# Low parts of the output weights: on TensorE with plus and minus identity instead of on GpSimd, in a block-sparse attention and feed-forward kernel

## The chip, the cores and the metric

The kernel runs on one core of a Trainium2 chip. The metric is the time of one execution on the device in microseconds (us). The engines are TensorE (PE; PEld is its loading of weights), VectorE (DVE), ScalarE (ACT), GpSimd (POOL) and SyncE (SP), which here issues loads and stores. Each has its own queue of instructions and works through it in order; semaphores tie the queues together. SBUF is the memory that all of them read and write, PSUM the one that TensorE writes its products to.

## The reference

Attention over 4 batches of 8 heads, 768 positions, head size 64, in which a position sees only some of the 24 blocks of 32 keys; then a feed-forward layer with a rational function, on 3072 tokens of 512 numbers, 2048 hidden. Inputs and results are float32.

```
scores = scale * q @ k.T;  scores = where(mask, scores, -1e9)     # mask: neighbours, first, last, 3 sampled blocks
attn = exp(scores - max) / sum;  x = attn @ v                      # x: (3072, 512)
h = x @ w_in                                                       # (3072, 2048)
P = a[0] + a[1]*h + a[2]*h*h + a[3]*h*h*h
Q = 1.0 + abs(b[0])*abs(h) + abs(b[1])*h*h
out = (P / (Q + 1e-06)) @ w_out                                    # (3072, 512)
```

The weights come as float64 words, 1024 words of 32 bits for 512 numbers, and the kernel makes float32 of them with integer instructions.

## The kernel before, in words

**Units.** The tokens are cut into 12 chunks of 256 and the hidden dimension into 8 units of 256, so there are 96 units (c, u). A unit first multiplies its chunk with its input weights on TensorE (`into`, lines 1040 to 1042, 24 products into a PSUM tile `ph`), then ScalarE and VectorE evaluate the rational function from `ph` (lines 1047 to 1085), of which line 1057 on VectorE is the last to read `ph`. Two tiles come of it: `gh`, and the small rest `gl`. TensorE multiplies them with the output weights into `acc` (lines 1097, 1099, 1103). The order of the units is written in line 399.

**Output weights in three parts.** Each of the 16 tiles (128 hidden rows, 512 columns) of the output weights is needed as `wo_h` (fp32r, high part, line 1097), `wo_l` (bf16, what is left of the number after the high part, line 1099) and `wo_b` (bf16, short copy, line 1103). `one` (lines 424 to 492) makes them: SP loads the words (`wl`, line 432), an engine converts them (line 442), VectorE packs them into float32 in `dw` with three instructions (lines 446, 449, 453), then `out_high` copies `dw` to `wo_h` (line 463), `out_low` subtracts `wo_h` from `dw` into `wo_l` (line 469) and `out_short` copies `dw` to `wo_b` (line 466). Copies run through the helper `times` (lines 147 to 154), and so carry its lines: 150 on ScalarE, 152 or 154 on VectorE, 154 on GpSimd. `dw` has three buffers, `wl` two. The two `wo` tiles hold words of the input weights before (`homes`), so the last parts of their tile can be written only when those have been used.

**Who does what.** `issue` (lines 164 to 269) plans the program when it is built: it holds a list of operations (`Op`) with an engine, or several to choose from (`among`), a price in ns, what they follow, a priority and the buffers that they take, and writes them out in the order that its simulated clock gives. So a changed price or engine of one operation can move others on every engine. `out_high` may go to ScalarE (520), GpSimd (588) or VectorE (335), `out_low` to GpSimd (1225) or VectorE (602; none goes there), `out_short` to ScalarE alone. `Slot` and `Ring` (lines 103 to 114) stand for buffers. `r_ph` (line 274) has two: the tiles of the pool `ps_h` (line 85), which the units' `ph` use in turn.

**Fill.** While the planner finds TensorE idle in the first 80 us of its clock, it issues a product that nobody reads (`fill`, line 162).

**Attention.** TensorE makes scores (line 821), turns the probabilities with the identity (line 898) and multiplies them with the values (line 944). In the first batch GpSimd copies sampled key blocks (line 765). SP issues all loads (values lines 916 to 923, keys 779 to 785, output weights 432). `ident` is the float32 identity, `ident16` its f16 copy (lines 91 to 94).

## Time and profile before

| | |
|---|---|
| time, median of 3 runs | 824.07 us (822.8 to 828.83) |
| time of the profiled execution | 823.95 us |
| its span, first to last instruction | 821.9 us |
| mean granted TensorE clock | 0.987 |
| PE busy | 779.4 us (95%) |
| DVE busy | 670.1 us (82%) |
| ACT busy | 570.7 us (69%) |
| POOL busy | 76.2 us (9%) |

Shares are means over stages that differ. A table of stretches gives the busy time of each engine in a part of the span. The clock is the share of full speed that TensorE was granted (two levels, 1.2 and 2.4 GHz, so a mean of 0.93 is a mixture of 1 and 0.5). In the lists of groups, "busy us, mean ns" are the sum and the mean of one instruction, and behind the second bar stands the idle time of the engine just before them, and what ended it.

### The profile page before, as it was taken

How to read it: one execution, taken by the hardware profiler on the slowest of the kernel's cores; microseconds unless marked ns; L12 is line 12 of the kernel's file. 1: busy time of each engine (PE TensorE's matmuls, PEld its weight loads, DVE VectorE, ACT ScalarE, POOL GpSimd, SP SyncE). 2: the span in 40 equal slices, each digit the busy share in tenths (PEclk: the TensorE clock that was granted, in tenths of full speed). 3: DMA queues.
4: the chain of work that ended last, by engine and by line, in shares of the span. 5: the costliest groups of instructions: out<-in, count | busy, mean ns of one | idle time of the engine just before them, and what ended most of it. 6: DMA issues, size and time to landing. Idle time of an engine off the chain costs nothing.

```text
span 821.9 us, 27500 instructions
## 1 busy us (share of the span) xinstructions
PE 779.4 (95%) x10947; PEld 558.8 (68%) x10947; DVE 670.1 (82%) x1569; ACT 570.7 (69%) x1263; POOL 76.2 (9%) x128
## 2 busy tenths in 40 slices
PE   7889868799999998999999999999999999999997
PEld 3557545566677767677777767677777767777774
DVE  3779999999988883988777875887788886887886
ACT  2578785966866868676776759675776758767563
POOL 3416341333000000000000000000000000000000
PEclk9999997999999999999999999999999999999999
DMA  8988977437556746536546756535555446220000
GB/s 218 224 216 248 260 184 215 131 115 193 151 147 190 213 128 196 153 112 171 150 125 184 181 152 193 145 98 156 145 153 148 117 130 173 67 65 2 1 26 26
DMA packets 224415, 121.29 MB, mean 148 GB/s; under 512 B 62624, under 2 KB 214048, under 8 KB 224288
## 3 DMA queue, kind: packets, MB, share of 16 engines
q1 hardware_dynamic: 223136, 115.34, 51.2%
q0 software_dynamic: 1152, 4.19, 1.7%
q8 instruction: 87, 1.43, 0.7%
q14 instruction: 40, 0.33, 0.1%
HBM read 108.47 MB, written 11.01 MB: 145 GB/s over the span
## 4 chain that ended last, share of the span: by engine, by line
PE 78%; DVE 13%; ACT 3%; DMA 2%; issue 2%; SPq 1%; ACTq 0%
PE acc L1097 10%; PE ph L1040 9%; PE acc L1103 9%; PE acc L1099 9%; PE ph L1041 9%; PE ph L1042 9%; PE m L821 6%; PE av L944 6%; PE m L898 5%; PE acc L162 2%; PE m L555 2%; DVE pr L833 1%; PE m L982 1%; DVE dw L449 1%; DMA vg<-in_v_dram 1%
## 5 line engine op out<-in xcount | busy, mean ns | idle before, releaser
L1040 PE MATMUL ph<-xh,wi 128*128 128x256 f16 x768 | 211.6, 276 | 7.9 <-DVE tt L1057 7.9
L1041 PE MATMUL ph<-xl,wi 128*128 128x256 f16 x768 | 211.2, 275 | 0.0
L1042 PE MATMUL ph<-xh,wi 128*128 128x256 f16 x768 | 211.2, 275 | 0.0
L1047 ACT ACTIVATE sq<-ph,fc 128x512 f32<-128x512 f32 x96 | 66.0, 687 | 116.4 <-PE ph L1042 116.4
L852 ACT ACTIVATE pr<-pr,st 128x256 f32<-128x256 f32 x224 | 110.8, 502 | 14.8 <-DVE st L864 14.7
L1097 PE MATMUL acc<-wo_h,gh 128*128 128x512 f32 x384 | 114.6, 420 | 1.5 <-DVE scw L361 0.8
L1064 DVE SCALAR_TENSOR_TENSOR ab<-sq,absb,ab 128x512 f32<-128x512 f32 x96 | 73.5, 766 | 37.1 <-ACT ab L1061 36.8
L1103 PE MATMUL acc<-wo_b,gl 128*128 128x512 bf16 x384 | 99.6, 382 | 2.2 <-DVE gl L1085 2.2
L1099 PE MATMUL acc<-wo_l,gh 128*128 128x512 bf16 x384 | 99.7, 382 | 0.0
L1040 PEld LDWEIGHTS <-wi 128*128 128x128 f16 x768 | 76.3, 99 | 24.3 <-issue 5.3
L1075 DVE SCALAR_TENSOR_TENSOR gh<-tt,par,rr 128x512 fp32r<-128x512 f32 x96 | 72.9, 761 | 21.0 <-ACT rr L1071 12.3
L1041 PEld LDWEIGHTS <-wi 128*128 128x128 f16 x768 | 75.8, 99 | 16.1 <-issue 4.0
L150 ACT ACTIVATE pT<-m 128x512 f32<-128x512 f32 x112 | 64.2, 595 | 30.3 <-PE m L898 29.0
L833 DVE CUSTOM_DVE_ANT_1 pr<-m,bias 128x256 f32<-128x256 f32 x204 | 76.2, 418 | 10.4 <-PE m L821 10.2
L1042 PEld LDWEIGHTS <-wi 128*128 128x128 f16 x768 | 75.8, 99 | 9.4
L1097 PEld LDWEIGHTS acc<-wo_h,gh 128*128 128x128 f32 x384 | 66.1, 191 | 15.0 <-issue 1.4
L1054 DVE TENSOR_TENSOR tt<-tt,sq 128x512 f32<-128x512 f32 x96 | 67.1, 699 | 9.9 <-ACT tt L1051 9.9
L1051 ACT ACTIVATE tt<-ph,par,fc 128x512 f32<-128x512 f32 x96 | 75.0, 781 | 0.1
L898 PE MATMUL m<-ident,pr 128*128 128x128 f32 x448 | 69.4, 286 | 4.7 <-ACT pT L150 4.0
L1061 ACT ACTIVATE ab<-ph,fc 128x512 f32<-128x512 f32 x96 | 65.7, 684 | 11.0 <-DVE tt L1081 10.4
L1081 DVE SCALAR_TENSOR_TENSOR tt<-tt,par,ab 128x512 f32<-128x512 f32 x96 | 72.8, 759 | 0.5
L1057 DVE SCALAR_TENSOR_TENSOR tt<-ph,fc,tt 128x512 f32<-128x512 f32 x96 | 71.5, 744 | 0.7
(136 smaller groups left out, 1195.7 us busy)
## 6 DMA issues: line engine op xcount, KB each, us to landing
vg<-in_v_dram SPq DMA_DIRECT2D x312, 64.0 KB, 2.7
vg<-in_v_dram SPq DMA_DIRECT2D x88, 192.0 KB, 3.3
kall<-ks SPq DMA_DIRECT2D x138, 64.0 KB, 2.0
wl<-in_moe_w_out_dram SPq DMA_DIRECT2D x16, 512.0 KB, 4.8
vg<-in_v_dram SPq DMA_DIRECT2D x12, 512.0 KB, 4.5
kall<-ks SPq DMA_DIRECT2D x23, 256.0 KB, 3.0
ldq<-in_q_dram SPq DMA_DIRECT2D x20, 256.0 KB, 3.6
out_dram<-ld SPq DMA_DIRECT2D x20, 256.0 KB, 2.3
```

Of the source, the lines that this page charges most:

```text
L833: nc.vector.tensor_tensor_reduce(out=prs[x][:, e, g].rearrange("p (s r) -> p s r", r=BLK), in0=h["sp"][g][:, e], in1=add.rearrange("p (s o ...
L852: nc.scalar.activation(out=prs[x][:, e, g], in_=prs[x][:, e, g], func=AF.Exp, scale=SCALE, bias=st[:, 12 + y:13 + y], accum_out=st[:, 16 + ...
L898: nc.tensor.transpose(pp[:, jj * P:(jj + 1) * P], pr[:, e, g, kt:NS * BLK:2], ident)
L1040: nc.tensor.matmul(o, wh, xh[:, :, cc], start=(cc == 0), stop=False)
L1041: nc.tensor.matmul(o, wh, xl[:, :, cc], start=False, stop=False)
L1042: nc.tensor.matmul(o, wl, xh[:, :, cc], start=False, stop=(cc == NCC - 1))
L1051: nc.scalar.activation(out=d["tt"], in_=d["ph"], func=AF.Identity, scale=d["cst"][:, 3:4], bias=par[:, 2:3])
L1064: nc.vector.scalar_tensor_tensor(out=d["ab"], in0=d["sq"], scalar=absb[:, 1:2], in1=d["ab"], op0=ALU.mult, op1=ALU.add)
L1075: nc.vector.scalar_tensor_tensor(out=d["gh"], in0=d["tt"], scalar=par[:, 0:1], in1=d["rr"], op0=ALU.add, op1=ALU.mult)
L1097: nc.tensor.matmul(acc, g, wo_h[:, f], start=(new and e == 0), stop=False)
L1099: nc.tensor.matmul(acc, g, wo_l[:, f], start=False, stop=False)
L1103: nc.tensor.matmul(acc, g, wo_b[:, f], start=False, stop=(last and e == 1))
```

## The change

A second constant `minus` holds minus the identity in fp32r. For all 16 tiles (`x < 16` holds for each) `wo_l` is now made in two steps: `split` on TensorE multiplies `dw` with the identity (float32) and `wo_h` with `minus` (fp32r) into one `ph` tile, and `out_rest` on ScalarE copies it from there to `wo_l`. The split takes one of the two buffers of `r_ph` and is priced at 1080. The short copy goes to GpSimd alone, and the price of a copy on GpSimd is 1050 instead of 588 for `out_high`.

```diff
+    minus = const.tile([P, P], F32R, name="minus")
+    nc.vector.tensor_scalar(out=minus, in0=ident, scalar1=-1.0, scalar2=None, op0=ALU.mult)
...
+            def split():
+                d["ps"] = ps_h.tile([P, 512], F32, name="ph")
+                nc.tensor.matmul(d["ps"], ident, d["w"].bitcast(F32), start=True, stop=False)
+                nc.tensor.matmul(d["ps"], minus, wo_h[:, x], start=False, stop=True)
+
+            def out_rest():
+                nc.scalar.activation(out=wo_l[:, x], in_=d["ps"], func=AF.Copy)
+
...
-                o1 = Op(among("o", SC, sc=520, po=588, ve=335), 0, out_high, [o], prio, uses=w)
-                o2 = Op(among("p", PO, po=1225, ve=602), 0, out_low, [o1] + homes(x), prio, uses=w)
-                o3 = Op(among("q", SC, sc=520, po=588, ve=335), 0, out_short, [o] + homes(x), prio, uses=w)
+                o1 = Op(among("o", SC, sc=520, po=1050, ve=335), 0, out_high, [o], prio, uses=w)
+                if x < 16:
+                    s_low = Slot(r_ph)
+                    o2 = Op(TE, 1080, split, [o1], prio, takes=[s_low], uses=w)
+                    o2 = Op(SC, 520, out_rest, [o2] + homes(x), prio, uses=[s_low])
+                else:
+                    o2 = Op(among("p", VE, ve=602), 0, out_low, [o1] + homes(x), prio, uses=w)
+                o3 = Op(among("q", PO, po=1050), 0, out_short, [o] + homes(x), prio, uses=w)
```

Over the whole program the instructions change so. PE: 16 products with `ident`, 16 with `minus`, 127 fill products instead of 139. ACT: 16 copies from `ph` to `wo_l`, none to `wo_b` (16 before), nine to `wo_h` (six before), three to `wi` from the words in `wo_b` (one before). POOL: no subtraction (16 before), 16 copies to `wo_b` (none), five to `wo_h` (ten), four to `wi` from the words in `wo_b` (six). DVE: two copies to `wo_h` (none), and the one that makes `minus`.

The planner writes the program anew behind the first tiles. On POOL, where the decoding of the output weights is in full swing, the queue before reads:

```order
L154 TENSOR_SCALAR wi<-wo_l 128x512
L154 TENSOR_SCALAR wo_h<-dw 128x512
L469 TENSOR_TENSOR wo_l<-dw,wo_h 128x512
L154 TENSOR_SCALAR wi<-wo_b 128x512
L154 TENSOR_SCALAR dw<-wl 128x512 x2
L469 TENSOR_TENSOR wo_l<-dw,wo_h 128x512
L154 TENSOR_SCALAR wo_h<-dw 128x512
```

and of the change (line 156 is the helper's line 154):

```order
L156 TENSOR_SCALAR wi<-wo_l 128x512
L156 TENSOR_SCALAR wo_b<-dw 128x512
L156 TENSOR_SCALAR wo_h<-dw 128x512
L156 TENSOR_SCALAR wi<-wo_b 128x512
L156 TENSOR_SCALAR dw<-wl 128x512 x2
L156 TENSOR_SCALAR wo_b<-dw 128x512 x2
L156 TENSOR_SCALAR wo_h<-dw 128x512
```

The subtraction behind each `wo_h` is gone, and a copy to `wo_b` stands ahead of `wo_h` in the queue.

On PE, after the first unit's last product with `wo_b` and ahead of the next unit's first product (`ld` is a tile of keys and `ldq` one of queries to be turned, `pr` a tile of probabilities), before:

```order
L1103 MATMUL acc<-wo_b,gl 128x512
L555 MATMUL m_103<-ident,ld 128x128 x4
L555 MATMUL m_104<-ident,ld 128x128 x4
L1040 LDWEIGHTS wi
L1040 MATMUL ph<-xh_117,wi 128x256
```

and of the change (lines 475 and 476 are the split, 570 answers to 555, 913 to 898, 1055 to 1040, 1118 to 1103):

```order
L1118 MATMUL acc<-wo_b,gl 128x512
L570 MATMUL m_106<-ident,ld 128x128 x8
L570 MATMUL m_104<-ident,ldq 128x128 x4
L475 MATMUL ph<-dw,ident 128x512
L476 MATMUL ph<-wo_h,minus 128x512
L913 MATMUL m_105<-ident,pr 128x128 x4
L475 MATMUL ph<-dw,ident 128x512
L476 MATMUL ph<-wo_h,minus 128x512
L570 MATMUL m_106<-ident,ld 128x128 x4
L913 MATMUL m_104<-ident,pr 128x128 x4
L1055 LDWEIGHTS wi
L1055 MATMUL ph<-xh_119,wi 128x256
```

These are the third and the fourth split; they take a `ph` buffer each, between two units that take one too, and turns that stood elsewhere have come between as well. The first eight splits stand before the fifth unit, the other eight between the tenth and the fourteenth.

On ACT the copies from the split stand between those of the attention. Before, at the first of these places (`pT` are turned probabilities, `sq`, `ab` and `tt` parts of a unit's function):

```order
L150 ACTIVATE wo_h<-dw 128x512
L150 ACTIVATE wo_b<-dw 128x512
L150 ACTIVATE pT<-m_102 128x512
L852 ACTIVATE pr,st<-pr,st 128x256 x4
L150 ACTIVATE pT<-m_102 128x512
L150 ACTIVATE wo_b<-dw 128x512
L1047 ACTIVATE sq<-ph,fc 128x512
```

and of the change (152 answers to 150, 867 to 852, 1062 to 1047; line 479 is `out_rest`):

```order
L152 ACTIVATE wo_h<-dw 128x512
L152 ACTIVATE pT<-m_104 128x512
L152 ACTIVATE dw<-wl 128x512
L479 ACTIVATE wo_l<-ph 128x512
L152 ACTIVATE pT<-m_104 128x512
L867 ACTIVATE pr,st<-pr,st 128x256 x4
L479 ACTIVATE wo_l<-ph 128x512
L1062 ACTIVATE sq<-ph,fc 128x512
```

Where a copy to `wo_b` stood, which needs only `dw`, there stands now a copy to `wo_l`, which needs a product of PE. A conversion that POOL made (`dw` from `wl`) has come to ACT here; over the whole program each of them has as many of those as before.

## Rows read from the trace of the kernel before

**Rows 1.** Stretch, length; busy us of PE, PEld, DVE, ACT, POOL; clock; DMA share, GB/s.

```profile
175.00:212.00 37.00, 35.16 (x585) 24.72 (x586) 37.00 (x82) 25.20 (x53) 13.32 (x11) 1.00 0.62 164
75.00:212.00 137.00, 115.15 (x1719) 82.58 (x1718) 134.32 (x284) 101.26 (x225) 48.23 (x51) 0.93 0.68 189
212.00:822.00 610.00, 601.98 (x8002) 436.11 (x7986) 487.40 (x1107) 424.96 (x926) 0.00 (x0) 1.00 0.47 130
```

**Rows 2.** Line 469: duration ns min/median/max, first and last start us.

```profile
L469 POOL TENSOR_TENSOR wo_l<-dw,wo_h x16: 1265/1484/1656, 67.6 to 208.6; 128x512 bf16<-128x512 f32 x16
```

**Rows 3.** Waits of PE, 75 to 212 us: total, times, longest.

```profile
PE ph L1040 <- DVE tt L1057: 7.9, 5, 2.5
PE m L898 <- ACT pT L150: 3.4, 1, 3.4
```

**Rows 4.** Groups by line over the whole span: count, busy us, mean ns.

```profile
L162 PE MATMUL acc<-ident 128*128 128x512 f16 x139 | 36.3, 393 | 1.7 <-DVE ident L94 1.7
L469 POOL TENSOR_TENSOR wo_l<-dw,wo_h 128x512 bf16<-128x512 f32 x16 | 23.3, 1453 | 12.7 <-ACT wo_h L150 11.9
L154 POOL TENSOR_SCALAR wo_h<-dw 128x512 fp32r<-128x512 f32 x10 | 10.5, 1054 | 34.9 <-DVE dw L453 28.5 <-DVE sc L360 4.9 <-DVE scw L352 1.4
L690 ACT ACTIVATE qt<-m 128x512 f32<-128x512 f32 x24 | 14.3, 597 | 10.8 <-PE m L555 10.7
L154 DVE TENSOR_SCALAR wi<-wo_l 128x512 f32<-128x512 f32 x1 | 0.9, 852 | 0.0
L154 DVE TENSOR_SCALAR wi<-wo_b 128x512 f32<-128x512 f32 x1 | 0.4, 396 | 0.0
```

**Rows 5.** POOL in order of time: start us, us, instruction [idle before].

```profile
98.36 1.59 POOL L154 TENSOR_SCALAR wo_h<-dw 128x512 fp32r<-128x512 f32 x1 [3.71 <-DVE dw L453]
...
107.34 1.33 POOL L469 TENSOR_TENSOR wo_l<-dw,wo_h 128x512 bf16<-128x512 f32 x1
...
208.59 1.29 POOL L469 TENSOR_TENSOR wo_l<-dw,wo_h 128x512 bf16<-128x512 f32 x1 [4.03 <-ACT wo_h L150]
```

**Rows 6.** DVE in order of time, at the same places.

```profile
99.40 1.09 DVE L1081 SCALAR_TENSOR_TENSOR tt<-tt,par,ab 128x512 f32<-128x512 f32 x1
...
107.46 1.77 DVE L1064 SCALAR_TENSOR_TENSOR ab<-sq,absb,ab 128x512 f32<-128x512 f32 x1
...
202.33 1.09 DVE L1075 SCALAR_TENSOR_TENSOR gh<-tt,par,rr 128x512 fp32r<-128x512 f32 x1
...
209.12 1.30 DVE L1085 TENSOR_TENSOR gl<-tt,rr 128x512 bf16<-128x512 f32 x1
```

**Rows 7.** Groups of DVE by line, 212 to 822 us.

```profile
L1064 DVE SCALAR_TENSOR_TENSOR ab<-sq,absb,ab 128x512 f32<-128x512 f32 x84 | 62.9, 749 | 36.5 <-ACT ab L1061 36.3
L1075 DVE SCALAR_TENSOR_TENSOR gh<-tt,par,rr 128x512 fp32r<-128x512 f32 x84 | 62.7, 747 | 21.0 <-ACT rr L1071 12.3 <-PE acc L1099 7.8 <-issue 0.6
L1081 DVE SCALAR_TENSOR_TENSOR tt<-tt,par,ab 128x512 f32<-128x512 f32 x84 | 62.6, 746 | 0.5
L1085 DVE TENSOR_TENSOR gl<-tt,rr 128x512 bf16<-128x512 f32 x84 | 57.4, 684 | 2.2 <-PE m L898 0.5
```

**Rows 8.** PE in order of time, at three places.

```profile
79.20 0.64 PE L898 MATMUL m<-ident,pr 128*128 128x128 f32 x4
79.67 0.27 PE L1040 MATMUL ph<-xh,wi 128*128 128x256 f16 x1
...
81.55 1.10 PE L944 MATMUL av<-vg,pT 128*32 128x64 f32 x64
82.58 1.09 PE L821 MATMUL m<-kall,qt 64*32 64x256 f32 x32
...
90.59 1.17 PE L1097 MATMUL acc<-wo_h,gh 128*128 128x512 f32 x4
91.60 1.04 PE L1099 MATMUL acc<-wo_l,gh 128*128 128x512 bf16 x4
```

**Rows 9.** A wait of POOL, 60 to 215 us: total, times, longest.

```profile
POOL dw L154 <- DMA wl<-in_moe_w_out_dram: 18.9, 7, 6.1
```

## The prediction

> **What bounds the kernel now.** I read the busy table by stretches first. From 212 us to the end TensorE (PE) is busy for 601.98 of 610 us, with the clock at 1.00: there only PE's work counts, and the change touches nothing there [rows 1]. From 75 to 212 us it is different. PE is busy 115.15 of 137 us, so it stands idle for 21.85 us, at a mean granted clock of 0.93, and VectorE (DVE) is busy 134.32 us, 98% [rows 1]. This is the stretch in which the weights are decoded, and 15 of the 16 low parts that the change rebuilds lie in it (the first starts at 67.6 us, the last at 208.6) [rows 2]. PE's waits say the same: 7.9 us for DVE's line 1057, which gives a `ph` buffer back, then single waits for ScalarE (ACT) copies [rows 3]. So DVE sets the pace until about 212 us, and PE does after. What PE has not done by then it does later at the same price. That gives two books to keep: DVE's work in the stretch, and PE's work plus PE's idle time over the whole span.
>
> **Removed: 16 subtractions on GpSimd (POOL).** They take 23.3 us of POOL, 1453 ns each [rows 4], and POOL is busy only 48 of the stretch's 137 us [rows 1], so POOL's own time is worth nothing. What they cost is on DVE. A subtraction runs from 107.34 us [rows 5]; the DVE instruction that starts at 107.46 takes 1.77 us [rows 6], where the same line takes 749 ns later, when POOL is silent [rows 7]. The last, at 208.59 us, makes line 1085 take 1.30 us instead of 684 ns. I went through the stretch this way, each DVE instruction against its line's later mean: under each of the 15 subtractions one is late, by 0.35 to 1.11 us, 13.6 us in all (the first at 76.09 us, the last at 209.12 us, shown).
>
> **Added on POOL: 16 copies with one input.** What such a copy does to DVE the trace shows too, since POOL makes 24 copies or conversions (line 154) in the stretch. Under 16 of them a DVE instruction is late, by 0.34 to 0.48 us, 6.4 us in all (first 76.83 us, last 202.33 us, 1.09 us against 747 ns) [rows 5 to 7]: 0.27 us per copy. After the change POOL makes 16 more of them, 5 fewer copies to `wo_h` and 2 fewer to `wi`, so 33 instead of 24: +2.4 us for DVE. DVE also gets two of the `wo_h` copies. It makes no such copy before; its conversions of 512 numbers took 0.40 and 0.85 us [rows 4], I take 0.7, so +1.4. **DVE's book: -13.6 + 2.4 + 1.4 = -9.8 us.**
>
> A rule speaks against this part. The Trainium skill (SBUF — State Buffer, the section on the shared port pair) says that a DVE instruction with two SBUF inputs and a GpSimd instruction that reads SBUF exclude each other, and that the loser waits for the winner's whole instruction. By the 1054 ns that a `wo_h` copy shows [rows 4], nine more copies would then cost DVE 9.5 us, and its book would be only -2.7. The trace agrees that one side stops, but not with the length: the copy of 1.59 us at 98.36 [rows 5] delayed DVE by 0.35 us [rows 6]; part of the copy's length is its own waiting. The rows decide, and the rule stays as a rival.
>
> **ACT** loses 16 copies to `wo_b` and gains 16 copies of the same size out of PSUM, two to `wi` and three to `wo_h`: +5 instructions at 0.6 us (a PSUM read of this size: 597 ns) [rows 4], +3 us. ACT is busy 101 of 137 us [rows 1], so I cost this at nothing; the cover is gone where a PE product waits for just such a copy, as the 3.4 us wait does [rows 3].
>
> **Added on PE: 16 pairs of products of 128x512.** The second has the form of line 1097: four steps from 90.59 to 91.60 us, 0.25 us each [rows 8]. The first multiplies plain f32, and no row shows one of this size. Lower bound: four turns of 128 f32 columns, 79.20 to 79.67 us, so 0.47 us for 512 columns. Upper bound: line 944, real f32 products: one part's 32 products fill four column strips, eight times 64 columns in each, and take from 81.55 to 82.58 us, 1.03 us for 512 columns [rows 8]. It is a product, not a turn, so I take 1.03. A pair is then 1.28 us and 16 are **20.5 us** (low end 0.72 and 11.6 us). Twelve fill products fall away (139 to 127); 36.3 us over 139 is 0.26 each [rows 4]: -3.1. **PE's book: +17.4 us.**
>
> **Where the 17.4 us can go.** PE's idle time in the stretch is 21.85 us. It can't all be filled: the densest part, 175 to 212 us, still leaves 37.00 - 35.16 = 1.84 us, 5% [rows 1]. At 5% of some 133 us, 6.6 us stay idle, so 15.3 us are absorbed. A fuller PE should also keep its clock. A mean of 0.93 over 137 us with two levels, full and half, is 2 x 0.07 x 137 = 19.2 us at half; at 84% busy that is 16.1 us of work, half of which, 8.1 us, comes back if the clock never falls. Where PE was 95% busy the clock was 1.00 [rows 1]; I take 6 of the 8.1 us.
>
> **Moved.** The order keeps the units of the second stage at the same places: the third and fourth split (a split: the two products for one tile) come just before the next unit's first product, as the rows in the section on the change show. New waits come with it: PE stands behind `wo_h`, which POOL now writes after a `wo_b` copy in some places, and each split takes one of the two `ph` buffers until ACT has read it. Behind a split that waits stand the turns and the next unit's products, and behind those ACT's and DVE's work on that unit. On SP's queue the loads of values, keys and output weights change places within the stretch. POOL waits for output weights, 18.9 us in seven times, 6.1 us at the longest [rows 9], and no load stands among PE's longest waits [rows 3]; I cost the new order at nothing, under the cover of tiles decoded ahead of their unit, and at up to those 6.1 us where the cover fails.
>
> **Sum.** Profiled execution 823.95 us (span 821.9 us, 2.05 us around it; median 824.07, so the two bases agree). 823.95 + 17.4 - 15.3 - 6 = **820 us**. It asks the stretch to shorten by 4 us, within the 9.8 us that DVE's book allows.
>
> **Rivals.**
> *DVE's relief comes through in full.* PE fits into a stretch shortened by 9.8 us: 814 us. For it: DVE at 98%, and the low end of the f32 price, which makes PE's book 8.5 instead of 17.4. Against it: at the price that I take, PE would have to run with 21.85 - 17.4 + 8.1 - 9.8 = 2.8 us of idle time, and that with the whole clock regained.
> *The splits wait themselves.* Each takes a `ph` buffer, and the wait for that buffer is already PE's largest (7.9 us over 5 times, 1.6 us each [rows 3]). If the 16 splits meet it at that mean, they bring 25 us of new waiting, more than what they fill; PE's idle then stays at about 21.85 us and the kernel pays the whole book less some 4 us of clock: 823.95 + 17.4 - 4 = 837 us. With my 6 us of clock it is slower by 8 us as soon as over 18.5 us of idle remain. For it: DVE frees the buffer late, since line 1057 waits its turn in a full queue. Against it: DVE has 9.8 us less to do.
> *Copies block as long as they run.* By the mechanism of the rule above, DVE gains 2.7 us, and the stretch can shorten by no more: 821 us. The rows speak against it; its time is within 1% all the same.
>
> **How the numbers follow.** About 1% (8 us) is what a measurement of this kernel can tell from no change. My forecast with its neighbours (816 to 830) 0.47, the rule's mechanism 0.04: same 0.51. Full relief 0.28: faster. Waiting splits 0.21: slower. The range has to reach both: 810 (full relief and the rest of the clock) to 834 (most of the waiting); the forecast's own range is 816 to 828.
>
> **What would show it.** DVE instructions beyond 1.5 us vanish, and those of 1.0 to 1.1 us stay; DVE's busy time falls by about 10 us. A split takes 1.28 us from its start to the next product. PE's idle time from 75 us to the point where it runs without a break falls to some 7 us, at a clock near 1.00. I am wrong if a split takes far less or more, if the copies to `wo_b` slow DVE as the subtractions did, or if PE shows waits for `ph` or `wo_h` at lines 475 and 476 of the changed kernel that add up to over 10 us.

## The result

The changed kernel is slower by 0.7%: 831.41 us as the median of 20 runs, where the kernel before, run beside it, has 825.53. The ratio is 1.0073, with a 95% interval of 1.0055 to 1.0091. On the 824.07 us shown ahead of the prediction that is 830.1 us: inside the range given (810 to 834), outside the forecast's own range (816 to 828), and on the other side of the time before. The single times of the changed kernel spread more than those of before (826.6 to 840.1 us against 820.8 to 829.5), and the ratio leaves out as slow its four runs above 839 us and one run of before at 1963 us. The other 16 take 826.6 to 836.8 us at mean granted clocks from 0.997 to 0.985. What follows goes by ratios, and by 825 us where they are turned into times. The profiled execution took 827.05 us.

The busy times of the whole span after, from the page:

```profile
PE 784.0 (95%) x10895; PEld 563.2 (68%) x10983; DVE 660.0 (80%) x1572; ACT 574.4 (70%) x1268; POOL 60.7 (7%) x121
```

The table of stretches after (start and end, length, then the busy time and the instruction count of each engine, the clock, the DMA share and GB/s):

```profile
75.00:212.00 137.00, 119.71 (x1733) 82.93 (x1744) 124.32 (x293) 105.35 (x236) 32.92 (x44) 0.99 0.66 184
75.00:156.00 81.00, 64.64 (x977) 44.43 (x980) 72.08 (x172) 64.38 (x146) 22.54 (x30) 0.98 0.71 202
156.00:175.00 19.00, 18.47 (x224) 13.04 (x232) 18.46 (x40) 13.84 (x31) 4.16 (x8) 1.00 0.54 157
175.00:212.00 37.00, 36.60 (x556) 25.46 (x544) 33.78 (x85) 27.13 (x62) 6.22 (x8) 1.00 0.64 160
212.00:825.00 613.00, 598.41 (x7906) 437.52 (x7979) 486.47 (x1102) 424.77 (x920) 0.00 (x0) 1.00 0.47 129
```

Beside [rows 1] this shows three things. DVE's busy time in 75 to 212 us fell from 134.32 to 124.32 us, by 10.0. The clock in that stretch rose from 0.93 to 0.99. But PE's idle time fell only from 21.85 to 17.29 us, and it lies elsewhere now: from 156 us on PE runs almost without a break (36.60 of 37 us from 175 to 212), while 16.36 of the 17.29 us stand in 75 to 156 us. The last row is short of some PE work because the trace lacks 71 of the 384 records of line 1114 and 17 of the 384 of line 1118.

The same two early stretches of the kernel before:

```profile
75.00:156.00 81.00, 63.53 (x980) 45.91 (x976) 78.49 (x167) 62.32 (x144) 29.78 (x36) 0.89 0.75 213
156.00:175.00 19.00, 16.45 (x156) 11.95 (x157) 18.83 (x38) 13.75 (x31) 5.13 (x5) 0.91 0.47 130
```

Up to 156 us PE's idle time is about what it was, 16.36 us after 17.47, although DVE is busy 6.4 us less: with DVE lighter, PE there didn't become fuller. It did more in the same busy time, at a clock of 0.98 instead of 0.89. The chain of waits between 85 and 133 us says what came instead (start, length, what). In the kernel before its long pieces here are all DVE's, up to 125 us. After the change it holds four landings of loads, 23.6 us of 48:

```profile
86.17 2.30 DMA vg<-in_v_dram
89.78 6.04 DMA ldq<-in_q_dram
...
100.56 5.14 DMA ld<-in_k_dram
...
121.88 10.14 DMA ld<-in_v_dram
```

Over the whole span the chain has this make-up, before and after the change:

```profile
PE 78%; DVE 13%; ACT 3%; DMA 2%; issue 2%; SPq 1%; ACTq 0%
PE 85%; DMA 5%; SPq 3%; issue 2%; ACT 2%; DVE 2%; ACTq 0%
```

PE's waits from 75 to 212 us after (line waited at, what for, us in total, times, longest), beside [rows 3]:

```profile
PE ph L1055 <- DVE tt L1072: 3.7, 2, 2.9
PE av L959 <- DMA vg<-in_v_dram: 1.9, 2, 1.6
PE m L913 <- ACT pr L867: 1.9, 1, 1.9
PE ph L475 <- DVE tt L1072: 1.8, 1, 1.8
```

The wait for `ph` at a unit's start was halved (7.9 to 3.7 us), and the splits (line 475) wait little: 1.8 us once.

The split, from PE's timeline, and the groups of the new work (mean ns of one record ahead of the second bar):

```profile
74.75 1.02 PE L475 MATMUL ph<-dw,ident 128*128 128x512 f32 x2
75.21 0.80 PE L476 MATMUL ph<-wo_h,minus 128*128 128x512 f32 x1
75.84 0.63 PE L913 MATMUL m<-ident,pr 128*128 128x128 f32 x4
...
109.45 1.10 PE L475 MATMUL ph<-dw,ident 128*128 128x512 f32 x2 [1.82 <-DVE tt L1072]
109.98 0.80 PE L476 MATMUL ph<-wo_h,minus 128*128 128x512 f32 x1
110.71 1.10 PE L959 MATMUL av<-vg,pT 128*32 128x64 f32 x64
```

```profile
L164 PE MATMUL acc<-ident 128*128 128x512 f16 x127 | 34.7, 408 | 1.7 <-DVE ident L94 1.7
L475 PE MATMUL ph<-dw,ident 128*128 128x512 f32 x32 | 17.1, 615 | 1.9 <-DVE tt L1072 1.8
L476 PE MATMUL ph<-wo_h,minus 128*128 128x512 f32 x16 | 12.7, 796 | 0.0
L156 POOL TENSOR_SCALAR wo_b<-dw 128x512 bf16<-128x512 f32 x16 | 16.4, 1026 | 68.4 <-DVE dw L455 60.2 <-DVE sc L362 4.3 <-DVE st L891 3.9
```

From its start to the next product a split takes 75.84 - 74.75 = 1.09 us of PE at the least and 110.71 - 109.45 = 1.26 us at the most, where no wait follows (13 of the 16; their mean is 1.15 us; the records overlap, so their sum is longer). 16 are some 18.4 us. Eight start between 74 and 120 us, eight between 165 and 208 us. Every product of PE in this trace goes to a PSUM tile and none to SBUF; the split's goes to `ph`, and ScalarE's copy brings it to `wo_l`.

### The profile page after: what moved, and what is told of

Its sections match the earlier page's. It is cut to its first block, busy times and chain, and to the rows that moved or that the text cites. A ratio compares the mean times of both kernels' runs of the same rounds, so it can differ in the third digit from the quotient of the medians.

```text
span 825.2 us, 27504 instructions
## 1 busy us (share of the span) xinstructions
PE 784.0 (95%) x10895; PEld 563.2 (68%) x10983; DVE 660.0 (80%) x1572; ACT 574.4 (70%) x1268; POOL 60.7 (7%) x121
## 4 chain that ended last, share of the span: by engine, by line
PE 85%; DMA 5%; SPq 3%; issue 2%; ACT 2%; DVE 2%; ACTq 0%
PE acc L1112 11%; PE ph L1055 10%; PE ph L1056 10%; PE ph L1057 10%; PE acc L1118 10%; PE acc L1114 9%; PE m L836 7%; PE av L959 6%; PE m L913 6%; PE acc L164 2%; PE m L570 2%; DMA ldq<-in_q_dram 2%; PE ph L475 1%; PE m L997 1%; DMA ld<-in_v_dram 1%
## 5 line engine op out<-in xcount | busy, mean ns | idle before, releaser
L1118 PE MATMUL acc<-wo_b,gl 128*128 128x512 bf16 x367 | 95.4, 379 | 3.6 <-issue 1.7
L1114 PE MATMUL acc<-wo_l,gh 128*128 128x512 bf16 x313 | 84.7, 380 | 4.7
L913 PEld LDWEIGHTS m<-ident,pr 128*128 128x128 f32 x448 | 62.9, 206 | 12.5 <-ACT pr L867 3.5
```

The lines of the kernel that those rows point to most:

```text
L913: nc.tensor.transpose(pp[:, jj * P:(jj + 1) * P], pr[:, e, g, kt:NS * BLK:2], ident)
L1114: nc.tensor.matmul(acc, g, wo_l[:, f], start=False, stop=False)
L1118: nc.tensor.matmul(acc, g, wo_b[:, f], start=False, stop=(last and e == 1))
```

## The experiments

All ratios are to the kernel before, run beside each kernel. A difference of two of them is known to about 0.3%, 2 to 3 us. The changed kernel itself stands at 1.0073.

### How long the products are

The first four kernels keep the changed kernel's order and change the length of a split alone. The first:

```diff
-                nc.tensor.matmul(d["ps"], ident, d["w"].bitcast(F32), start=True, stop=False)
+                nc.tensor.matmul(d["ps"], minus, wo_h[:, x], start=True, stop=False)
```

> The changed kernel in its own order of instructions, but in all 16 splits the plain f32 product (identity times the scaled words) is replaced by a second fp32r product of minus identity with the high part, so the low parts hold other numbers. A split should take some 0.50 us instead of the 1.09 us seen in the changed kernel, so PE has 16 x 0.59 = 9.4 us less to do. Theory 1 (a split that lies where PE never stands idle costs its whole length; one that lies between PE's waits costs part of it): the eight late splits (165 to 208 us) give back 8 x 0.59 = 4.7 us in full, the eight early ones (74 to 120 us) 0 to 3 us: ratio to the kernel before 0.998 to 1.002 where the changed kernel has 1.0073. Theory 2 (the loss is in new waits for the ph buffers and in the changed order, not in the length of the products): 1.006 to 1.008.

Measured: 0.9998 [0.9977, 1.0019]. A cheap split takes 0.61 us in the mean of the 12 that no wait follows, so PE has 8.7 us less. 6.2 us came through, so the length of the products matters, and it is not all in waits for buffers.

The second and third make the same edit only where `x >= 8`, and only where `x < 8`.

> As the run with all splits cheap, but only the eight late splits (x from 8 on, 165 to 208 us) have the cheap first product; their low parts hold other numbers. Theory 1: 8 x 0.59 = 4.7 us less, the whole of it seen in the time: ratio 1.001 to 1.003. Theory 2: 1.006 to 1.008. A third theory, that PE's length counts the same everywhere because later waits shift along: the same gain here as in the run where the early eight are cheap.

Measured: 1.0108 [1.0066, 1.0151], not below the changed kernel. In its profile PE waits where the time was to be saved, 2.6 us at the unit's first product around 200 us for a copy out of `ph`, and 1.1 us at a split:

```profile
PE ph L1058 <- ACT wo_l L482: 2.6, 1, 2.6
PE ph L476 <- DVE tt L1075: 1.1, 1, 1.1
```

The same profile loses time far behind the splits as well: at 509 us PE has waited 2.6 us for a load of values, and right behind that the granted clock falls to half. So this run's time is not the price of the late splits alone.

```profile
PE av L962 <- DMA vg<-in_v_dram: 2.6, 1, 2.6
```

> The eight early splits alone (x below 8, 74 to 120 us) have the cheap first product; their low parts hold other numbers. Theory 1: PE stands idle 16 to 17 us between 70 and 160 us in the changed kernel, so most of the 4.7 us becomes more waiting: ratio 1.004 to 1.007. Theory 2: 1.006 to 1.008. The third theory (length counts everywhere): 1.001 to 1.003, as with the late eight.

Measured: 1.0057 [1.0023, 1.0092]. The two halves don't add up to the run with all 16, and with these intervals they can't tell the early half from the late. What they do refute is my first theory in its simple form: a PE that is full from 156 us on does not give back what is taken from it there, where theory 1 had 1.001 to 1.003 for the late half. That decoded tiles and buffers come hardly earlier than PE needs them is my reading of the two waits; it was not tried apart.

The fourth adds a second plain product to each split:

```diff
                 nc.tensor.matmul(d["ps"], ident, d["w"].bitcast(F32), start=True, stop=False)
+                nc.tensor.matmul(d["ps"], ident, d["w"].bitcast(F32), start=False, stop=False)
```

> The other direction: each split does its plain f32 product twice, so the low parts hold other numbers and a split takes some 0.84 us more. Theory 1: the late eight cost 6.7 us in full, the early eight 1 to 4 us: 8 to 11 us more than the changed kernel, ratio 1.017 to 1.021. The third theory (length counts everywhere): 13.4 us, ratio 1.0235. Theory 2 (waits and order, not length): under 3 us more, ratio below 1.011.

Measured: 1.0109 [1.0083, 1.0134]. Some 13.8 us more for PE cost 3.0 us. That is in the range of theory 2 and refutes the other two. In the profile most of the new work went into idle time: from 75 to 156 us PE is busy 72.04 us, 7.4 more than in the changed kernel, at the same clock.

```profile
75.00:156.00 81.00, 72.04 (x1027) 49.16 (x1033) 73.00 (x173) 64.86 (x147) 23.52 (x31) 0.98 0.73 205
```

The mean granted clock of its runs is 0.995, where the changed kernel has 0.992 and the kernel before 0.985, so a smaller part may have come back through the clock.

### What the relief of VectorE is worth

The changed kernel with no product at all in the splits:

```diff
             def split():
-                d["ps"] = ps_h.tile([P, 512], F32, name="ph")
-                nc.tensor.matmul(d["ps"], ident, d["w"].bitcast(F32), start=True, stop=False)
-                nc.tensor.matmul(d["ps"], minus, wo_h[:, x], start=False, stop=True)
+                pass
...
-                nc.scalar.activation(out=wo_l[:, x], in_=d["ps"], func=AF.Copy)
+                nc.scalar.activation(out=wo_l[:, x], in_=wo_h[:, x].bitcast(F32), func=AF.Copy)
```

> The changed kernel in its own order, but the splits issue no products at all: ScalarE copies the high part into the place of the low part, so the low parts hold other numbers. All 17.4 us of PE's new work are gone and no split takes a ph buffer; VectorE's relief and GpSimd's new copies stay. What is left is the worth of the relief alone. If the relief counts in full, as the prediction's book of VectorE had it: 9.8 us below the kernel before, ratio 0.986 to 0.989. If loads set the stretch from 85 to 132 us once VectorE no longer does (the trace of the changed kernel has a chain of landings there), and the decoded tiles themselves come late near 200 us: ratio 0.994 to 0.999, little below the 0.9998 of the run in which all splits were cheap.

Measured: 1.0009 [0.9988, 1.0030]. This is the run that turned the question round. DVE is relieved by 11.8 us over the span (658.3 us busy, 670.1 before), PE has no new work, and nothing is gained. So the products, with their waits for `ph`, cost 1.0073 - 1.0009 = 0.64%, 5.3 us of their 18.4, and the loss has a second part. Their price is not in proportion to their length: the cheap splits of the first run, 9.7 us, cost nothing beside this run (0.9998 against 1.0009), the next 8.7 us cost 6.2 and the next 13.8 cost 3.0, each to some 2.5 us.

Delays brought back to DVE in the changed kernel:

```diff
-                times(eng, wo_b[:, x], d["w"].bitcast(F32), 1.0)
+                eng.tensor_tensor(out=wo_b[:, x], in0=d["w"].bitcast(F32), in1=d["w"].bitcast(F32), op=ALU.add)
```

> The changed kernel in its own order, but GpSimd makes the 16 short copies with two inputs (the scaled words added to themselves, so the short copies are doubled in value), a form that delays VectorE as the subtractions did. Splits stay. VectorE's busy time from 75 to 212 us should rise by 16 x 0.6 = about 10 us again. If the relief of VectorE counts in full: 8 to 10 us above the changed kernel, ratio 1.017 to 1.020. If loads set the pace in 85 to 132 us and PE from 156 us on: only part of it, ratio 1.008 to 1.014.

Measured: 1.0084 [1.0055, 1.0114]. This settled little: DVE's busy time over the span rose only by 3.6 us (660.0 to 663.6), not by 10.

Then DVE's own work, made less and more in the kernel before, whose order stays (one of three packing steps left out, or one done twice):

```diff
             def pack2():
+                if kind:
+                    return
```

> The kernel before in its own order, with one of VectorE's three packing steps left out for the 16 output-weight tiles (so these weights hold other numbers): 16 x 0.68 = 10.9 us less work for VectorE, about the relief that the change was to bring, with nothing added anywhere. Theory A (VectorE sets the pace from 75 to 212 us, as the prediction had it): 9 to 11 us less, ratio 0.987 to 0.990. Theory B (as soon as VectorE is lighter, loads, tiles handed from engine to engine and a lower clock of a PE that waits take its place): 0.994 to 1.000. Theory C (the changed kernel's order is what is bad, and in the order of before the relief would count): as A.

Measured: 0.9921 [0.9890, 0.9952].

```diff
             def pack3():
...
+                if kind:
+                    nc.vector.scalar_tensor_tensor(out=to, in0=d["words"][:, :, 1], scalar=-2 ** 31, in1=d["w"], op0=ALU.bitwise_and, op1=ALU.bitwise_or)
```

> The kernel before in its own order, with the third packing step done twice for the 16 output-weight tiles (the second time changes nothing): 16 x 0.68 = 10.9 us more for VectorE. Theory A: 9 to 11 us more, ratio 1.011 to 1.013. Theory B: VectorE is one of several limits that lie close together, so more of its work still counts: 1.007 to 1.013; a ratio below 1.005 would say that VectorE did not set the pace even in the kernel before.

Measured: 1.0142 [1.0106, 1.0178]. DVE's work counts in the kernel before, in both directions: 10.9 us less bring 6.5, 10.9 more cost 11.7. The gain is 60% of theory A's; 0.9921 lies between the ranges of A and B, and its interval touches both, so B's other limits are not excluded. (A step left out also brings each tile sooner; that was not told apart from DVE's busy time.) In the changed kernel the first of the two edits, the same two lines in `pack2`, gives less:

> The changed kernel with one packing step of VectorE left out for the 16 output-weight tiles (these weights hold other numbers): 10.9 us less for VectorE, as in the run made of the kernel before (0.9921, a gain of 0.79%). If VectorE still sets the pace of the changed kernel: the same gain, ratio 0.998 to 1.001. If PE is full from 156 us on and loads and hand-overs hold the time before: ratio 1.003 to 1.008.

Measured: 1.0039 [1.0015, 1.0063], a gain of 2.8 us of 10.9, where the kernel before gained 6.5. Each of the two gains is known to some 2.5 us, so they are only just apart: after the change the time seems to hang less on DVE.

Loads, the next suspect, with no products in the splits:

```diff
-                    nc.sync.dma_start(out=d["ld"], in_=wo64[x * P:(x + 1) * P])
+                    nc.sync.dma_start(out=d["ld"][:, 0:WC], in_=wo64[x * P:(x + 1) * P, 0:WC])
```

> As the run without any product in the splits (1.0009), and besides each output-weight tile loads only half its bytes (each engine reads that half twice, so its instructions keep their sizes; the weights hold other numbers). If the loads of these tiles are what holds the stretch once VectorE is lighter: 0.992 to 0.997. If they are not (the waits are between the engines, or for the other loads): 0.999 to 1.003.

Measured: 0.9976 [0.9950, 1.0002]. Half of the bytes of 16 loads bring 2.7 us, at the edge of what can be told; these loads are a small part of the answer at most. The loads that stand in the chain above are others, of queries, keys and values; no run changed those. (Only the load is shown; the instructions that read the tile are edited too, so that they read the half twice.)

### Old and new order

If relief counts in the kernel before and nothing comes of it in the changed one without products, either the new order or the new work itself eats it. Two kernels make the missing corners of a table. In the first, the order of before keeps its places, and only what stands in them changes:

```diff
             def out_short(eng):
-                times(eng, wo_b[:, x], d["w"].bitcast(F32), 1.0)
+                eng.activation(out=wo_l[:, x], in_=d["w"].bitcast(F32), func=AF.Copy)
...
             def out_low(eng):
-                eng.tensor_tensor(out=wo_l[:, x], in0=d["w"].bitcast(F32), in1=wo_h[:, x].bitcast(F32), op=ALU.subtract)
+                times(eng, wo_b[:, x], d["w"].bitcast(F32), 1.0)
```

> The kernel before in its own order, but GpSimd makes the short copies in the places of its subtractions, and ScalarE makes a copy of the same size into the low part in the places of its short copies (so the low parts hold other numbers); no split on PE. It is the change without PE's part, in the old order; the same work in the new order gave 1.0009. If the new order is what eats VectorE's relief: 0.991 to 0.996 here, as the run with 10.9 us less for VectorE (0.9921). If the relief itself is worth nothing (a delay under GpSimd hides behind other waits, or the new copies cost as much): 0.998 to 1.002.

Measured: 0.9910 [0.9887, 0.9933].

The second puts the subtraction into the places of the short copies of the changed order, and leaves the products out:

```diff
             def out_short(eng):
-                times(eng, wo_b[:, x], d["w"].bitcast(F32), 1.0)
+                nc.gpsimd.tensor_tensor(out=wo_l[:, x], in0=d["w"].bitcast(F32), in1=wo_h[:, x].bitcast(F32), op=ALU.subtract)
...
             def out_rest():
-                nc.scalar.activation(out=wo_l[:, x], in_=d["ps"], func=AF.Copy)
+                nc.scalar.activation(out=wo_b[:, x], in_=wo_h[:, x].bitcast(F32), func=AF.Copy)
```

> The other corner: the changed kernel's order with the work of before. GpSimd subtracts in the places of the short copies (three of the 16 later, where the high part is not there yet), ScalarE makes the short copy in the place of its copy out of PSUM, the splits issue nothing. If the new order costs what the relief brings: 1.006 to 1.010 (the relief of 6 to 7 us taken away from 1.0009). If the order is neutral and the relief worth nothing: 0.999 to 1.003.

Measured: 1.0110 [1.0083, 1.0137]. The table, without products on PE in any of the four:

| | order of before | order of the change | what the order costs |
|---|---|---|---|
| work of before | 1.0000 | 1.0110 | 9.1 us |
| work of the change | 0.9910 | 1.0009 | 8.2 us |
| what the relief brings | 7.4 us | 8.3 us | |

Both orders agree on the relief, and both kinds of work agree on the order (the two differences are 0.9 us apart, with an error of some 3). The relief is worth 7 to 8 us, where DVE's book had 9.8. The new order costs 8 to 9 us, and the prediction had it at nothing. With the products' 5.3 us the sum is -8.3 + 9.1 + 5.3 = +6.1 us, and the changed kernel stands at +6.0; that has to come out, since the three are steps of one path from the kernel before to the changed one. The order here is the whole plan: with it go twelve fill products fewer and the copies to `wo_h` and `wi` that changed engines. And in the new order ScalarE's 16 copies read `wo_h`, in the old one `dw`; in the profiles of the three kernels measured here ScalarE shows no wait at those copies.

The busy times of the first, the second and the run without products, in this order, show that the work is as meant: DVE is 10.4 us lighter than before in the first, 1.0 in the second, 11.8 in the third.

```profile
PE 771.5 (95%) x10863; PEld 558.7 (69%) x10947; DVE 659.7 (81%) x1569; ACT 571.4 (70%) x1263; POOL 69.8 (9%) x128
```

```profile
PE 774.7 (93%) x10848; PEld 558.5 (67%) x10935; DVE 669.1 (81%) x1572; ACT 573.8 (69%) x1268; POOL 74.2 (9%) x121
```

```profile
PE 780.4 (95%) x10935; PEld 557.5 (68%) x10935; DVE 658.3 (80%) x1572; ACT 573.8 (70%) x1268; POOL 64.2 (8%) x121
```

Up to 156 us the order makes little difference to PE's idle time. With the new work it is 16.21 us in the old order and 16.53 in the new, beside 17.47 in the kernel before:

```profile
75.00:156.00 81.00, 64.79 (x995) 47.47 (x997) 78.39 (x181) 66.82 (x158) 26.97 (x37) 0.92 0.76 218
```

```profile
75.00:156.00 81.00, 64.47 (x1043) 46.68 (x1033) 73.90 (x181) 66.87 (x154) 27.26 (x37) 0.92 0.74 217
```

Where the order costs shows in the stretch from 156 to 232 us, new work in the old order first, then the same work in the new one, then old work in the new one:

```profile
156.00:232.00 76.00, 75.00 (x1092) 55.89 (x1099) 70.79 (x163) 57.90 (x123) 14.73 (x15) 1.00 0.61 163
```

```profile
156.00:232.00 76.00, 69.64 (x1024) 48.52 (x1023) 68.37 (x153) 56.49 (x122) 9.62 (x10) 1.00 0.54 153
```

```profile
156.00:232.00 76.00, 66.77 (x957) 47.21 (x961) 71.52 (x155) 55.88 (x124) 20.28 (x18) 0.98 0.56 154
```

In the old order PE, rid of the late DVE, runs 75.00 of 76 us. In the new order it stands idle for 6.4 us with the same kinds of work, and DVE isn't full either (68.37 of 76): PE waits for single hand-overs, from DVE above all, none of them long. For the run without products, in that stretch:

```profile
PE m L911 <- DVE ab L1077: 1.6, 1, 1.6
PE m L834 <- DVE st L846: 1.5, 1, 1.5
PE m L995 <- DVE xn L983: 1.4, 2, 1.2
PE acc L1116 <- DVE gl L1098: 1.2, 1, 1.2
```

That is 5.4 us more than in the old order, of the 8.2 that the order costs with this work; where the rest lies the profiles do not show. It is lost early: ScalarE's first instruction on the 26th unit starts at 286.8 us in the old order and at 296.0 in the new, 9.2 us later, and the two spans differ by 10.1. That the late splits are cheap fits this: the products fill gaps that the new order has there anyhow (PE's idle time from 156 to 212 us is 0.93 us in the changed kernel).

Which of the moved instructions make the gaps was not tried. A candidate that the waits name (ScalarE, 67 to 225 us, old order, then the new one with the same work) is ScalarE's copy to `wo_h`, of which the new plan gives it nine instead of six, since a copy on GpSimd is priced at 1050:

```profile
ACT wo_h L150 <- DVE dw L453: 2.5, 3, 1.5
```

```profile
ACT wo_h L152 <- DVE dw L455: 8.9, 6, 2.5
```

A run with that price alone is missing.

Another order of the same work:

```diff
-                    o2 = Op(TE, 1080, split, [o1], prio, takes=[s_low], uses=w)
+                    o2 = Op(TE, 1300, split, [o1], prio, takes=[s_low], uses=w)
```

> The changed kernel with one number of the planner altered: a split is planned at 1300 ns instead of 1080. The work is the same, only the order in which the planner puts it differs. If the order alone is worth several us: a ratio more than 0.004 away from 1.0073, either way. If not: 1.004 to 1.010.

Measured: 1.0088 [1.0066, 1.0110]. This plan is no better; a difference of 1.2 us to the changed kernel is within the error. So a second plan of the same work does not win either. That the order of before is an uncommonly good one, so that most new plans lose against it, would fit too; it was not tried.

### The change in the old order, and parts of it

If the order costs so much, the whole change in the old order should be fast, unless the splits cost more there. Here pairs of products (`split_now`) and ScalarE's copies (`rest_now`, at the latest ahead of the next user of `ph`) are put between the planned instructions:

```diff
+        while owed and not held and r_ph.free:
+            split_now(*owed.pop(0), te)
...
+            while held and r_ph in o.rings:
+                rest_now()
```

> The whole change (products on PE, ScalarE's copy out of PSUM, short copies on GpSimd), computing what the reference wants, but in the order of the kernel before: GpSimd's short copy stands where its subtraction stood, and the 16 pairs of products and 16 copies are put between the planned instructions without the planner knowing of them, as soon as a ph buffer is free; three pairs stand directly ahead of the products that read their result. If the order is what made the change slower: 0.991 for the relief plus 0.0064 for the products, that is 0.995 to 0.999. If the order is not the cause: 1.005 to 1.010. The just-in-time pairs may add 1 to 4 us.

Measured: 1.0209 [1.0171, 1.0246]: 24.7 us above the same work without products (0.9910). The expectation failed. PE's longest wait, and the total wait of ScalarE's copies for their products (67 to 225 us):

```profile
PE ph L170 <- DVE tt L1081: 6.5, 3, 5.8
```

```profile
ACT wo_l L176 <- PE ph L171: 20.6, 10, 9.2
```

A split that the plan doesn't know waits 5.8 us for a `ph` buffer that DVE gives back late, and ScalarE stands 9.2 us behind it with everything that it does for the units. In the changed kernel the same row reads

```profile
ACT wo_l L479 <- PE ph L476: 3.6, 4, 1.8
```

So the old order has no room for the splits at the places where this kernel puts them, and putting them in so costs more than planning anew. Whether other places would do is open.

The same for the early tiles alone:

```diff
             def out_low(eng):
-                times(eng, wo_b[:, x], d["w"].bitcast(F32), 1.0)
-                owed.append((x, d))
+                if x < 8:
+                    times(eng, wo_b[:, x], d["w"].bitcast(F32), 1.0)
+                    owed.append((x, d))
+                else:
+                    eng.tensor_tensor(out=wo_l[:, x], in0=d["w"].bitcast(F32), in1=wo_h[:, x].bitcast(F32), op=ALU.subtract)
```

> As the run with the whole change in the old order, but for the eight early tiles alone; the eight late ones keep GpSimd's subtraction and ScalarE's short copy. About half of the relief (0.45%) stays, and half of the products go, the half that lies where PE is full. If late products cost their whole length and early ones little: 0.993 to 0.997, below the run with all 16. If the relief of the late tiles counts for more than their products: above it, 0.997 to 1.001.

Measured: 1.0127 [1.0094, 1.0160], 10.5 us slower than before. The wait of 5.8 us is among the first eight splits, and stays.

Three kernels that are planned anew, with a part of the change each. VectorE makes the low parts (the kernel before with one name changed):

```diff
-                o2 = Op(among("p", PO, po=1225, ve=602), 0, out_low, [o1] + homes(x), prio, uses=w)
+                o2 = Op(among("p", VE, ve=602), 0, out_low, [o1] + homes(x), prio, uses=w)
```

> The kernel before with one line changed: VectorE makes the low parts, not GpSimd; nothing on PE, short copies stay on ScalarE. VectorE is rid of 13.6 us of delays and gets 16 subtractions of 0.68 us, 10.9 us: 2.7 us less. If VectorE's own time sets the stretch from 75 to 212 us in full: ratio 0.996 to 0.998. If loads are close behind: 0.998 to 1.002.

Measured: 1.0018 [1.0002, 1.0035].

The change for the eight early tiles, with the late ones' work as before, or with the late ones' low parts on VectorE, which is this one line alone:

```diff
-                if x < 16:
+                if x < 8:
```

> The change for the eight early tiles (x below 8) alone: split by PE, short copy by GpSimd. The eight late tiles as in the kernel before (subtraction on GpSimd, short copy on ScalarE). The program's order is planned anew from these costs. If a split costs little between 74 and 120 us, where PE stands idle, and much where PE is full: the full PE of the late stretch is left alone, ratio 0.996 to 1.002. If a split costs its length anywhere: 8.7 us of new work less some clock, ratio 1.003 to 1.006.

Measured: 0.9990 [0.9966, 1.0015].

> The change for the eight early tiles by PE, and for the eight late tiles the low part on VectorE (0.68 us each); all 16 short copies on GpSimd; the order is planned anew. Against the changed kernel PE has 8 x 1.09 = 8.7 us less where it is full, VectorE 5.5 us more where it has 3 us of idle time (175 to 212 us). If PE's late splits are what made the change slower: ratio 0.997 to 1.002, as the run with the early eight alone (0.999). If VectorE is the next limit there: 1.002 to 1.006.

Measured: 1.0019 [0.9987, 1.0051]. Each has its own order, so these three can't be read as the worth of a part; they show that no split of the work tried here beats the kernel before. The two kernels that are clearly faster, 0.9910 and 0.9921, leave work out.

## Why the prediction failed

**What bounds the kernel now: right in the main.** DVE sets the pace of the kernel before in the stretch: leaving out 10.9 us of its work there brings 6.5 us, adding as much costs 11.7. With less work for DVE other limits come close: 60% of the saving came through.

**Removed and added on POOL: right, and by the mechanism given.** DVE's busy time in the stretch fell by 10.0 us where the book said 9.8; its seven instructions beyond 1.5 us, one of them in [rows 6], are gone, and some of 1.0 to 1.1 us stay. The copies to `wo_b` delayed DVE by 5.6 us, 0.35 each, in the old order (the sum over the DVE instructions that lie under one), and by 1.5 to 2.9 us in the changed kernel, since half of the eight late instructions there lie under another GpSimd instruction as well; 0.27 each was taken. So the book came out closer than its terms. The rival by which DVE waits as long as a copy runs is refuted: DVE would have lost over 9 us to them. The relief is worth 7.4 to 8.3 us of time.

**Added on PE: two errors that cancel in part.** A split takes 1.15 us instead of 1.28, so 18.4 us instead of 20.5: between the bounds of 0.72 and 1.28, nearer the upper one that was taken. The fill products saved 1.6 us (36.3 to 34.7), not 3.1: 0.13 us for each of the twelve that fell away, where the mean over all [rows 4] had been taken. PE's book was 16.8 us instead of 17.4.

**Where the 17.4 us can go: the term that missed.** The sum had 15.3 of 21.85 us of idle time absorbed. Measured, idle time fell by 4.6 us; from 75 us to where PE runs without a break it is 16.9 us, where some 7 were forecast. With the sizes measured the prediction's own sum reads 823.95 + 16.8 - 4.6 - 4.6 = 831.6, beside the 830.1 that came (the idle time is that of the one profiled execution, 827.05 us), so this term carries the miss. The argument took the 5% of one dense stretch, 175 to 212 us, and gave it to the whole of 75 to 212; but what PE does in a stretch also hangs on what reaches it there. From 75 to 156 us the idle time went from 17.47 to 16.36 us, with loads in the chain in DVE's place; that the loads hold it is not shown, and longer splits did fill a part of it.

**Moved: the step that failed.** "I cost the new order at nothing", with 6.1 us as its upper end. The table of four puts it at 8.2 and 9.1 us. The rest of the forecast, 3.9 us below the time before, agrees with the relief and the products as measured (-8.3 + 5.3 = -3.0 us). Had the term been +9.1 on the forecast of 820, it would have read 829, next to the 830.1 that came. This and the idle time are two views of one loss, not to be added. One thing stays open: the products' 5.3 us were measured in the new order, whose gaps they fill; in an order without gaps they may cost more, so it is not shown that the change would win in a better plan. The cover that I named, tiles decoded ahead of their unit, was no cover: what was lost are hand-overs between DVE, ScalarE and PE from 156 to 232 us, where the old order leaves PE 1.0 us of idle time and the new one 6.4 with the same work.

**Clock: right.** The clock in the stretch rose to 0.99, and over the runs from a mean of 0.985 to 0.992. Over the 16 runs of the changed kernel 0.01 of mean clock goes with 6.6 us, so this is an estimated 4.6 us; 6 were taken.

**The rivals.** The full relief (814) failed on the order: without products and in the old order the ratio is 0.9910, 816.7 us, so the relief exists; with the products no plan or run has it. The splits that wait themselves (837) did not come about as told: PE's waits for line 475 are 1.8 us, not 25. But the mechanism is real, as the splits put into the old order show (1.0209); the planner, which keeps account of the `ph` buffers, placed the splits without it. That making room for them is what the new order pays for would fit, but is not shown. Of the three signs named for being wrong none came: a split was near its price, the copies slowed DVE less than the subtractions had, and the waits at lines 475 and 476 are 1.8 us. None of them could show the price of a new order; the idle time of 16.9 us instead of 7 did.

## What to carry to other kernels

Where a planner writes the program, a change has three prices: its work, the work that it relieves, and the new order. The first two could be read here from the trace before to 2 or 3 us of engine time. The third could not, so it belongs in the range with a size of its own (here 1% of the time), and not at nothing. The test that isolates it is cheap: put the new work into the old places, and the old work into the new places, and read the four times as a table. What such a table calls the order is the whole plan, and the price of work that PE gets is the price in that plan.

Idle time of an engine is not room for any work (here 18.4 us of products cost 5.3, and idle time fell by 4.6 all the same): ask for each stretch what would reach the engine if the wait at the end of its idle time were gone.

## What was unexpected of the hardware

A GpSimd copy with one input can be the side that waits. In the changed kernel six of the 16 copies to `wo_b` take 0.61 or 0.62 us; one took 3.47, while DVE ran five instructions with two SBUF inputs without a pause, each at its usual length:

```profile
98.67 3.47 POOL L156 TENSOR_SCALAR wo_b<-dw 128x512 bf16<-128x512 f32 x1 [4.44 <-DVE dw L455]
```

```profile
98.52 0.73 DVE L1096 SCALAR_TENSOR_TENSOR tt<-tt,par,ab 128x512 f32<-128x512 f32 x1
99.18 0.67 DVE L1069 TENSOR_TENSOR tt<-tt,sq 128x512 f32<-128x512 f32 x1
99.78 0.68 DVE L1100 TENSOR_TENSOR gl<-tt,rr 128x512 bf16<-128x512 f32 x1
100.38 0.68 DVE L455 SCALAR_TENSOR_TENSOR wo_b<-wo_b,wi 128x512 int32<-128x512 int32 x1
100.98 0.68 DVE L451 SCALAR_TENSOR_TENSOR wi<-wo_l,wi 128x512 int32<-128x512 int32 x1
```

The Trainium skill (SBUF — State Buffer, SBUF: two separate sides) has the side that starts first hold the shared port pair for its whole instruction, while the other fully blocks. Here the trace agrees with that for GpSimd as the loser, and over several instructions of the winner (no run tried another cause of the 3.47 us), while DVE lost at most 0.46 us to such a copy, less than the 0.61 us that the copy takes alone.

More work on PE cost much less than its length, and the granted clock rose with it: 18.4 us of products cost 5.3 (mean clock of the runs 0.984 without them, 0.992 with them), and 13.8 us more cost 3.0 (0.995). At 6.6 us for 0.01 of clock, an estimate from the 16 runs above, the clock gave back some 5 and 2 us of that; in the second case PE's idle time from 75 to 156 us fell by 7.4 us.
